# Sliding-window scores of two heads per matmul: 64x64 tiles, queries spread block-diagonally, and one buffer of exponentials

## The chip, the cores and the metric

The kernel runs on one core of one Trainium2 chip. A core has a matrix engine (TensorE, "PE" in the profile, with its weight loads "PEld"), VectorE ("DVE"), ScalarE ("ACT"), GpSimd ("POOL") and SyncE ("SP", which issues most DMAs). Each engine runs its own list of instructions in order and waits on semaphores for the others. Matrix products land in PSUM, eight banks of 512 float32 columns on 128 partitions; all else lives in SBUF. The metric is the time of one execution in microseconds on the device; the time before is the median of three runs.

## The reference

Two attention blocks read the same input `x` (2048 positions, 1024 features, 32 heads of 32) and are mixed by a gate per position:

```python
g = sigmoid((x * gate_w).sum(-1, keepdims=True))
# block A: linear attention; phi(t) = where(t > 0, t + 1, exp(t)) + 1e-6
kv = einsum("bhsd,bhse->bhde", phi(k), v);  z = phi(k) summed over positions
a  = (phi(q) @ kv) / (phi(q) . z + 1e-6)            # then @ A_wo
# block B: each position looks at W = 8 positions, 2 apart, back from itself
logits = q . k[pos - 2*w] * 32**-0.5                # -1e9 where pos - 2*w < 0
b  = softmax(logits) @ v[pos - 2*w]                 # then @ B_wo
out = g * a + (1 - g) * b
```

The change lies in block B, in the product of queries and keys ahead of the softmax.

## The kernel before

The kernel builds a list of operations (`P.op`: engine, function, modelled cost, tiles read and written) and a planner orders it. The planner (`schedule`) runs through modelled time: on each engine it takes, among the operations that are ready, the one with the lowest priority number, which mostly is the order of the program's text. A read-out of PSUM marked "any" (`move`) goes to whichever of ScalarE and VectorE would finish it first by the model. The whole plan is made six times, each with PSUM banks chosen by the plan before, and the one with the shortest modelled span is kept. The order on each engine is then fixed; semaphores follow from the tiles that operations share.

Positions are stored so that even and odd ones form two halves of 1024 (`HS`), so that the window of every second position becomes a window of eight neighbours. The stages, in order of TensorE: values of block B for all positions, written to HBM (`vB_hbm`); queries and keys of block B (`qT`, `kT`, features on partitions, four heads of 32 on the 128 partitions of each of eight chunks), first for one half of the positions, then for the other; key features of block A (`pkS`, `phi`); the products of key features with `x` (line 1628, into `mT`) and from them the state of block A (`state`, line 1607); query features, the fold of the state into the output weights (`fold`, line 1655); and last the output products (line 1700), one tile of 128 positions after another.

The sliding window is worked off beside these stages, in 18 fills (nine of each half of the positions). A fill covers 114 queries (112 in the last of a half) as two sets of `nq` = 57 or 56; each set has its own 64 keys, on partitions 0 to 63 and 64 to 127 of the result. `slot` is called after each main group of eight full matmuls and starts a fill each fifth time (`FILL` = 0.2); the fill's values follow at least three slots later (`PVLAG`). A fill is this:

- two DMAs bring the values of its keys into `vt`;
- `s_fn`, the scores: for each of eight chunks, two sets and four heads one matmul of 32 rows (the head's features), 64 columns (keys) and 57 moving columns (queries), 64 in all, head `j` of a chunk into bank `SO[j]`, that is PSUM banks 4 to 7;
- ScalarE takes the exponential of all four banks into `E` (one of two buffers, `Er`), VectorE multiplies `E` by a mask that keeps the eight keys of each query;
- `values`: 64 matmuls of 64 rows, 32 columns, 57 moving columns from `E` into banks 4 and 5, and after the third chunk eight matmuls with a matrix of ones, 456 moving columns each, for the sums of the softmax, into banks 6 and 7;
- the sums' reciprocal by ScalarE (logarithm, then exponential), and VectorE's product, which overwrites the fill's own queries in `qT`.

Since scores, values and sums all use banks 4 to 7, a fill's scores wait until VectorE has read the result of the fill before. The main groups have banks 0 to 3 (0 to 2 from line 1596 on). [...]

Of the kernel before, what the change touches and what calls it, by code (L numbers as in the profile page):

```python
# [6 lines left out]
ACT = mybir.ActivationFunctionType  # L7
ALU = mybir.AluOpType
AX = mybir.AxisListType
BF16 = mybir.dt.bfloat16  # L10
F32 = mybir.dt.float32
# [1108 lines left out]
def build_kernel(nc, A_x, A_wqkv, A_wo, B_x, B_wqkv, B_wo, gate_w, out):  # L1120
    del B_x
    S = A_x.shape[1]
    NT = S // 128
    HS = S // 2
# [6 lines left out]
    def SB(shape, dtype, name, at=None):  # L1131
        n = SZ[dtype]
        for d in shape[1:]:
            n *= d
        if at is None:
            at = base[0]
            base[0] += (n + 31) // 32 * 32
        uid[0] += 1
        h = nc.alloc_sbuf_tensor_at("%s_%d" % (name, uid[0]), list(shape), dtype, offset=at)
        return Tile("S", h, at, list(shape), dtype)  # L1140
# [48 lines left out]
    def hb(p0, p1, half):  # L1189
        return [("H%d" % half, p0, p1, None)]  # L1190

    xT = SB([128, 8, S], BF16, "xT")
    qT = SB([128, 8, S], BF16, "qT")
    kT = SB([128, 8, S], BF16, "kT")
# [16 lines left out]
    zb = SB([128, 1024], BF16, "zb")  # L1211
    denr = Ring([SB([128, H], F32, "den%d" % i) for i in range(2)])
    mx4 = SB([128, 3], F32, "mx4")
    mx1 = SB([1, 3], F32, "mx1")
    flag = SB([1, 1], I32, "flag")
    zs = SB([128, 16], F32, "zs")
# [4 lines left out]
    vst = Ring([SB([128, 512], BF16, "vst%d" % i) for i in range(8)])  # L1221
    top_ = base[0]
    base[0] = ph
    Er = Ring([SB([128, 32 * 57], BF16, "E%d" % i) for i in range(2)])
    Lr = Ring([SB([128, 2, 4 * 57], F32, "L%d" % i) for i in range(2)])
    vr = Ring([SB([128, 1024], BF16, "v%d" % i) for i in range(3)])
    mtmp = [SB([128, 2, 57], BF16, "mt%d" % i, at=vr.t[2].lo + 256 * i) for i in range(2)]
# [27 lines left out]
    act = lambda n: 0.19 + n / 1200.0  # L1255
    dps = lambda n: 0.14 + n / 960.0

    def plan(seen):

        P = Prog(nc, nc.alloc_semaphore)  # L1260
# [23 lines left out]
        def C(eng, fn, cost, writes, reads=()):  # L1284
            return P.op(eng, fn, cost, reads=reads, writes=writes, prio=-1)

        C("pool", lambda e: e.memset(ones[:], 1.0), 0.1, [ones.all()])
        for i, (n, offs) in enumerate(KINDS):
            for h, o in enumerate(offs):
                m = mtmp[h]  # L1290
                b0 = o + 64 * h
                C("pool", lambda e, m=m: e.memset(m[:], 1.0), 0.1, [m.all()])

                C("pool", lambda e, m=m, n=n, b0=b0: e.affine_select(out=m[:, :, 0:n], in_=m[:, :, 0:n], compare_op=ALU.is_ge, fill=0.0, base=b0,
                                                                     pattern=[[0, 2], [1, n]], channel_multiplier=-1), 0.3, [m.all()], [m.all()])
                C("pool", lambda e, m=m, n=n, b0=b0: e.affine_select(out=m[:, :, 0:n], in_=m[:, :, 0:n], compare_op=ALU.is_ge, fill=0.0, base=7 - b0,
                                                                     pattern=[[0, 2], [-1, n]], channel_multiplier=1), 0.3, [m.all()], [m.all()])
                C("dve", lambda e, m=m, n=n, h=h, i=i: e.tensor_copy(msk[i][64 * h:64 * h + 64, :, :], m[64 * h:64 * h + 64, :, 0:n]), 0.2, [msk[i].all()], [m.all()])
                P.ops[-1].prio = 1100
# [100 lines left out]
        for t, half, lo, hi in [p for q in steps for p in q]:  # L1400
# [6 lines left out]
            if hi < 8:  # L1407
# [4 lines left out]
                 writes=[hb(t * 128, (t + 1) * 128, half)], chan="vst%d" % vs, lat=0.5, prio=5)  # L1412
# [15 lines left out]
        SO = banks[4:8]  # L1428
        main = Pool(banks[0:4])
        todo = []  # L1430
        later = []
        masks = []
        slot_n = [0]

        def fill(e_, qs, nq, offs):
            t0 = e_ * HS
            k0 = [qs + nq * h - offs[h] for h in range(2)]
            m = msk[KINDS.index((nq, offs))]
            vt, vslot = vr.next()
            for h in range(2):  # L1440
                P.op("sp", lambda e, h=h: e.dma_start(vt[64 * h:64 * h + 64, :], vB_hbm[t0 + k0[h]:t0 + k0[h] + 64, :]), 0.4,
                     reads=[hb(t0 + k0[h], t0 + k0[h] + 64, i) for i in range(2)], writes=[vt.all()], chan="v%d_%d" % (vslot, h), lat=0.5)

            def s_fn(e):
                for c in range(8):
                    for h in range(2):
                        for j in range(4):
                            last = e.matmul(SO[j].ap(c * nq, (c + 1) * nq)[64 * h:64 * h + 64, :], kT[32 * j:32 * j + 32, c, t0 + k0[h]:t0 + k0[h] + 64],  # L1448
                                            qT[32 * j:32 * j + 32, c, t0 + qs + h * nq:t0 + qs + (h + 1) * nq], start=True, stop=True, tile_position=(32 * j, 64 * h))
                return last  # L1450
            P.op("pe", s_fn, 0.65, mode="r", reads=[kT.part((0, 8), (t0 + k0[0], t0 + k0[1] + 64)), qT.part((0, 8), (t0 + qs, t0 + qs + 2 * nq))],
                 writes=[s.iv for s in SO], name="S")
            E, _ = Er.next()
            P.op("act", lambda e: e.activation(E[:, 0:32 * nq].rearrange("p (j q) -> p j q", j=4), ps[:, 4:8, 0:8 * nq], ACT.Exp), act(32 * nq),  # L1454
                 reads=[s.iv for s in SO], writes=[E.all()])
            ev = lambda: E[:, 0:32 * nq].rearrange("p (g q) -> p g q", g=16)
            mk = P.op("dve", lambda e: e.tensor_tensor(ev(), ev(), m[:, :, :].rearrange("p r q -> p (r q)")[:, None, :].to_broadcast([128, 16, 2 * nq]), ALU.mult),  # L1457
                 0.15 + 32 * nq / 1920.0, reads=[E.all(), m.all()], writes=[E.all()])
            masks.append(mk)

            def values():

                def each(e):
                    for c in range(8):
                        for j in range(4):
                            for h in range(2):
                                hd = 4 * c + j
                                last = e.matmul(SO[h].ap(c * nq, (c + 1) * nq)[32 * j:32 * j + 32, :], vt[64 * h:64 * h + 64, hd * 32:hd * 32 + 32],  # L1468
                                         E[64 * h:64 * h + 64, (8 * j + c) * nq:(8 * j + c + 1) * nq],
                                         start=True, stop=True, tile_position=(64 * h, 32 * j))  # L1470
                        if c == SUMS_AT:
                            for j in range(4):
                                for h in range(2):
                                    e.matmul(SO[2 + h].ap(0, 8 * nq)[32 * j:32 * j + 32, :], ones[64 * h:64 * h + 64, 0:32],  # L1474
                                             E[64 * h:64 * h + 64, 8 * j * nq:8 * (j + 1) * nq],
                                             start=True, stop=True, tile_position=(64 * h, 32 * j))
                    return last
                bi = [s.iv for s in SO]
                P.op("pe", each, 0.66, mode="c", reads=[vt.all(), ones.all(), E.all()], writes=bi, name="PV")
                for g in range(2):  # L1480
                    L, _ = Lr.next()
                    pb = lambda o, g=g: ps[:, 4 + 2 * o:6 + 2 * o, 4 * g * nq:4 * (g + 1) * nq]
                    P.op("act", lambda e, L=L, pb=pb: e.activation(L[:, :, 0:4 * nq], pb(1), ACT.Ln), act(8 * nq), reads=[SO[2].iv, SO[3].iv], writes=[L.all()])
                    P.op("act", lambda e, L=L: e.activation(L[:, :, 0:4 * nq], L[:, :, 0:4 * nq], ACT.Exp, scale=-1.0), act(8 * nq), reads=[L.all()], writes=[L.all()])  # L1484
                    P.op("dve", lambda e, L=L, pb=pb, g=g: e.tensor_tensor(  # L1485
                        qT[:, 4 * g:4 * g + 4, t0 + qs:t0 + qs + 2 * nq].rearrange("p c (h q) -> p h c q", h=2),
                        pb(0).rearrange("p h (c q) -> p h c q", c=4), L[:, :, 0:4 * nq].rearrange("p h (c q) -> p h c q", c=4), ALU.mult), dps(8 * nq),
                        reads=[SO[0].iv, SO[1].iv, L.all()], writes=[qT.part((4 * g, 4 * g + 4), (t0 + qs, t0 + qs + 2 * nq))])
            after(PVLAG, values)
# [12 lines left out]
        def after(n, f, cols=False):  # L1502
            later.append((slot_n[0] + n, f, cols))
            later.sort(key=lambda x: x[0])
# [245 lines left out]
    for _ in range(PASSES):  # L1750
        got = plan(seen)
        seen = got[2]
        if best is None or got[0].span < best[0].span:
            best = got
    P, flag_op = best[:2]
# [40 lines left out]
def bass_gated_mix__linear_attn_block__sliding_local_dilated__prompt_kernel(nc, A_x, A_wqkv, A_wo, B_x, B_wqkv, B_wo, gate_w, out):  # L1796
    return build_kernel(nc, A_x, A_wqkv, A_wo, B_x, B_wqkv, B_wo, gate_w, out)
# [28 lines left out]
```

## Time and profile before

| | |
|---|---|
| median of three runs | 486.28 us (486.14 to 486.35) |
| profiled execution | 485.35 us, of which the span is 483.5 us |
| granted TensorE clock | 1.0 |
| TensorE busy | 480.0 us, 99% of the span |
| VectorE, ScalarE, GpSimd busy | 294.9, 146.9, 39.4 us |
| score groups | 18, between 125.2 and 306.2 us |

A row of the time line gives start, length, engine, line of the kernel, operation, output and inputs, shape and count; a row of a group gives busy time, mean duration in ns, and the idle time before it with what ended it. Shapes of matmuls read rows*columns of the array, then partitions x moving columns. A matmul's end is modelled, so a chain of TensorE pieces is best priced from start to start. Neighbouring instructions of a line are merged in one row.

### The profile page before, as it was taken

To read this page: it belongs to the slowest core of one execution; us is meant where nothing else is said; L and a number is where in the kernel's file an instruction comes from. 1 tells how busy PE (TensorE), PEld (TensorE's weight loads), DVE (VectorE), ACT (ScalarE), POOL (GpSimd) and SP (SyncE) were. 2 spreads that over 40 slices of the span, in tenths; PEclk is the share of its full clock that TensorE was granted. 3 is DMA by queue.
4 is the path that set the end of the run, shared out by engine and by line. 5 is a ranking of instruction groups with operands and counts; after the bars stand their busy time and mean duration, and the time that the engine had idled before them with its cause. 6 is when DMAs were issued, how large, how long until landed. Compare 5 with 4: busy or idle time off the path is not lost.

```text
span 483.5 us, 10963 instructions
## 1 busy us (share of the span) xinstructions
PE 480.0 (99%) x4882; PEld 229.0 (47%) x4882; DVE 294.9 (61%) x490; ACT 146.9 (30%) x229; POOL 39.4 (8%) x40
## 2 busy tenths in 40 slices
PE   9999999999999999999999999999999999999997
PEld 6444444444444444444455555444444444444444
DVE  2212186799777778766733222489987777767522
ACT  2111111112344446666654356264222000011000
POOL 3000000000000000000015757010000000000000
DMA  8999996223100032013004340571234111122111
GB/s 243 203 190 322 340 342 188 81 94 107 26 23 26 25 110 73 27 34 111 24 25 122 129 104 4 132 197 24 65 89 87 45 43 45 44 66 66 45 45 48
DMA packets 73977, 48.51 MB, mean 100 GB/s; under 512 B 38337, under 2 KB 67394, under 8 KB 73922
## 3 DMA queue, kind: packets, MB, share of 16 engines
q1 hardware_dynamic: 73090, 46.94, 35.5%
q10 hardware_dynamic: 832, 0.79, 0.8%
q8 instruction: 40, 0.66, 0.6%
q14 instruction: 15, 0.12, 0.1%
HBM read 30.41 MB, written 8.39 MB: 80 GB/s over the span
## 4 chain that ended last, share of the span: by engine, by line
PE 99%; DVE 0%; issue 0%
PE ps_all L1349 58%; PE ps_all L1700 23%; PE ps_all L1628 12%; PE ps_all L1448 2%; PE ps_all L1468 2%; PE ps_all L1385 1%; PE ps_all L1474 1%; PE ps_all L1607 1%; PE ps_all L1655 0%; DVE o L1379 0%
## 5 line engine op out<-in xcount | busy, mean ns | idle before, releaser
L1349 PE MATMUL ps_all<-w,xT 128*128 128x512 bf16 x512 | 112.9, 379 | 0.0
L1349 PE MATMUL ps_all<-xT,w 128*128 128x512 bf16 x512 | 112.2, 379 | 0.0
L1349 PEld LDWEIGHTS ps_all<-xT,w 128*128 128x128 bf16 x512 | 49.3, 98 | 58.7
L1349 PEld LDWEIGHTS ps_all<-w,xT 128*128 128x128 bf16 x512 | 49.0, 98 | 57.6
L1355 ACT ACTIVATE e<-ps_all 128x512 bf16<-128x512 f32 x64 | 38.2, 597 | 109.5 <-PE ps_all L1349 108.7
L1700 PE MATMUL ps_all<-w,qT 128*128 128x512 bf16 (+1 forms) x264 | 60.7, 373 | 0.0
L1700 PE MATMUL ps_all<-kT,aT 128*128 128x512 bf16 (+1 forms) x264 | 60.7, 373 | 0.0
L1349 PE MATMUL ps_all<-kT,xT 128*128 128x512 bf16 x256 | 57.9, 379 | 0.0
L1628 PE MATMUL ps_all<-pk,xn 128*128 128x512 bf16 x256 | 57.8, 380 | 0.0
L1700 PEld LDWEIGHTS ps_all<-w,qT 128*128 128x128 bf16 x264 | 25.8, 98 | 29.6 <-issue 0.2
L1700 PEld LDWEIGHTS ps_all<-kT,aT 128*128 128x128 bf16 x264 | 25.8, 98 | 29.4
L1349 PEld LDWEIGHTS ps_all<-kT,xT 128*128 128x128 bf16 x256 | 24.7, 98 | 30.0 <-issue 0.7
L1376 DVE CAST vst<-ps_all 128x512 bf16<-128x512 f32 x16 | 11.1, 692 | 45.4 <-PE ps_all L1349 45.4
L1628 PEld LDWEIGHTS ps_all<-pk,xn 128*128 128x128 bf16 x256 | 23.9, 98 | 27.4
L1379 DVE TENSOR_SCALAR o<-ps_all,gm 128x512 bf16<-128x512 f32 (+1 forms) x27 | 19.7, 731 | 28.0 <-PE ps_all L1700 28.0
L1356 DVE TENSOR_SCALAR e<-e 128x512 bf16<-128x512 bf16 x64 | 18.8, 296 | 27.5 <-ACT e L1355 27.2
L1454 ACT ACTIVATE E<-ps_all 128x1824 bf16<-128x1824 f32 (+1 forms) x18 | 30.4, 1688 | 15.8 <-PE ps_all L1448 15.1
L1457 DVE TENSOR_TENSOR E<-E,msk 128x1824 bf16<-128x1824 bf16 (+1 forms) x18 | 19.8, 1103 | 23.3 <-ACT E L1454 23.3
L1590 POOL TENSOR_TENSOR zacc<-zacc,pk 128x1024 f32<-128x1024 f32 x15 | 32.0, 2130 | 16.5 <-DVE E L1457 15.7
L1485 DVE TENSOR_TENSOR qT<-ps_all,L 128x456 bf16<-128x456 f32 (+1 forms) x36 | 21.2, 625 | 19.4 <-ACT L L1484 19.2
L1377 ACT ACTIVATE kT<-ps_all 128x512 bf16<-128x512 f32 x25 | 14.2, 599 | 33.6 <-PE ps_all L1349 33.6
L1377 ACT ACTIVATE vst<-ps_all 128x512 bf16<-128x512 f32 x16 | 9.6, 597 | 48.7 <-PE ps_all L1349 48.7
(63 smaller groups left out, 361.0 us busy)
## 6 DMA issues: line engine op xcount, KB each, us to landing
v<-vB_hbm SPq DMA_DIRECT2D x36, 128.0 KB, 2.6
vB_hbm<-vst SPq DMA_DIRECT2D x32, 128.0 KB, 4.9
w<-in_B_wqkv_dram SPq DMA_DIRECT2D x4, 1024.0 KB, 8.4
xt<-in_A_x_dram SPq DMA_DIRECT2D x16, 256.0 KB, 5.3
w<-in_A_wqkv_dram SPq DMA_DIRECT2D x4, 1024.0 KB, 9.7
xn<-in_A_x_dram SPq DMA_DIRECT2D x8, 512.0 KB, 3.7
out_dram<-o SPq DMA_DIRECT2D x15, 256.0 KB, 2.1
kT<-in_A_wqkv_dram SPq DMA_DIRECT2D x2, 1024.0 KB, 5.6
```

The costliest lines, as they stand in the source:

```text
L1349: last = e.matmul(bank.ap(), lhs(dc), rhs(dc), start=(dc == 0), stop=(dc == 7))
L1355: P.op("act", lambda e: e.activation(e_[:, :], bank.ap(), ACT.Exp), act(512), reads=[bank.iv], writes=[e_.all()])
L1356: P.op("dve", lambda e: e.tensor_scalar(e_[:, :], e_[:, :], 1.0, 1e-6, op0=ALU.min, op1=ALU.add), 0.25, reads=[e_.all()], writes=[e_.all()])
L1376: fd = lambda e: e.tensor_copy(dst, src())
L1377: fa = lambda e: e.activation(dst, src(), ACT.Copy)
L1379: fd = lambda e: e.tensor_scalar(dst, src(), scale, None, op0=ALU.mult)
L1454: P.op("act", lambda e: e.activation(E[:, 0:32 * nq].rearrange("p (j q) -> p j q", j=4), ps[:, 4:8, 0:8 * nq], ACT.Exp), act(32 * nq), rea ...
L1457: mk = P.op("dve", lambda e: e.tensor_tensor(ev(), ev(), m[:, :, :].rearrange("p r q -> p (r q)")[:, None, :].to_broadcast([128, 16, 2 * n ...
L1485: P.op("dve", lambda e, L=L, pb=pb, g=g: e.tensor_tensor(qT[:, 4 * g:4 * g + 4, t0 + qs:t0 + qs + 2 * nq].rearrange("p c (h q) -> p h c q" ...
L1590: P.op("pool", lambda e, t=t: e.tensor_tensor(zacc[:, :], zacc[:, :], pkS[:, t, :], ALU.add), 2.2, reads=[src, zacc.all()], writes=[zacc.a ...
L1628: last = e.matmul(bank.ap(), tl[:, t, cs:cs + 128], pkS[:, t, r * 512:(r + 1) * 512], start=(t == 0), stop=(t == NT - 1))
L1700: last = e.matmul(bank.ap(0, f1 - f0), lh[:, k, t * 128:(t + 1) * 128], w[:, k, f0:f1], start=(first and k == 0), stop=(not first and k == 7))
```

## The change

A matmul now takes two heads at once: 64 rows (the features of two neighbouring heads), 64 columns (keys), 114 moving columns. So that the two heads are not added up, the queries are first spread into a buffer `qx` of two layers: layer 0 holds the queries with the odd heads of each pair set to zero, layer 1 with the even heads set to zero. The moving operand is the 57 queries of a set from layer 0 and then the same 57 from layer 1, two runs, so one matmul gives the scores of both heads, side by side. There are 32 such matmuls a fill, on four tiles of 64x64.

The spreading (`spread`) is a copy by ScalarE with a scale per partition (column 0 of `pick`, ones and zeros) and a multiplication by VectorE (column 1 of `pick`), each of 8 x 114 columns on 128 partitions. It is put into the list right after the mask of the fill before, and for a fill that has none before it, ahead of its own scores. `qx` is one buffer. Its size is that of one `E`, and `Er` has one buffer instead of two. The heads lie in another order in `E` and in the score banks (pair of heads, chunk, head of the pair): the values' matmuls read other addresses, and the sums' moving operand is eight runs of 57 columns instead of one of 456. The modelled cost of a score group goes from 0.65 to 0.6 us. `pick` is made once, by five memsets on VectorE.

```diff
-    Er = Ring([SB([128, 32 * 57], BF16, "E%d" % i) for i in range(2)])
+    Er = Ring([SB([128, 32 * 57], BF16, "E")])
+    qx = SB([128, 2, 8, 2 * 57], BF16, "qx")
...
+        C("dve", lambda e: e.memset(pick[:, :], 0.0), 0.1, [pick.all()])
+        P.ops[-1].prio = 1100
+        for i in range(4):
+            C("dve", lambda e, i=i: e.memset(pick[32 * i:32 * i + 32, i % 2:i % 2 + 1], 1.0), 0.1, [pick.all()], [pick.all()])
+            P.ops[-1].prio = 1100
...
+        ready = []
+
+        def spread(e_, qs, nq, offs):
+            ready.append((e_, qs))
+            rd = [pick.all(), qT.part((0, 8), (e_ * HS + qs, e_ * HS + qs + 2 * nq))]
+            to = lambda i: qx[:, i, :, 0:2 * nq]
+            of = lambda: qT[:, :, e_ * HS + qs:e_ * HS + qs + 2 * nq]
+            P.op("act", lambda e: e.activation(to(0), of(), ACT.Copy, scale=pick[:, 0:1]), act(16 * nq), reads=rd, writes=[qx.part((0, 1), (0, 8), (0, 114))])
+            P.op("dve", lambda e: e.tensor_scalar(to(1), of(), pick[:, 1:2], None, op0=ALU.mult), 0.1 + 16 * nq / 1920.0, reads=rd, writes=[qx.part((1, 2), (0, 8), (0, 114))])
...
+            if (e_, qs) not in ready:
+                spread(e_, qs, nq, offs)
...
-                        for j in range(4):
-                            last = e.matmul(SO[j].ap(c * nq, (c + 1) * nq)[64 * h:64 * h + 64, :], kT[32 * j:32 * j + 32, c, t0 + k0[h]:t0 + k0[h] + 64],
-                                            qT[32 * j:32 * j + 32, c, t0 + qs + h * nq:t0 + qs + (h + 1) * nq], start=True, stop=True, tile_position=(32 * j, 64 * h))
+                        for g in range(2):
+                            last = e.matmul(SO[2 * g + c // 4].ap(c % 4 * 2 * nq, (c % 4 + 1) * 2 * nq)[64 * h:64 * h + 64, :], kT[64 * g:64 * g + 64, c, t0 + k0[h]:t0 + k0[h] + 64],
+                                            qx[64 * g:64 * g + 64, :, c, h * nq:(h + 1) * nq], start=True, stop=True, tile_position=(64 * g, 64 * h))
...
+            if todo:
+                spread(*todo[0])
...
-                                         E[64 * h:64 * h + 64, (8 * j + c) * nq:(8 * j + c + 1) * nq],
+                                         E[64 * h:64 * h + 64, (j // 2 * 16 + 2 * c + j % 2) * nq:(j // 2 * 16 + 2 * c + j % 2 + 1) * nq],
...
-                                             E[64 * h:64 * h + 64, 8 * j * nq:8 * (j + 1) * nq],
+                                             E[64 * h:64 * h + 64, j // 2 * 16 * nq:(j // 2 + 1) * 16 * nq].rearrange("p (c s q) -> p c s q", c=8, s=2)[:, :, j % 2, :],
```

More of the change, by code (lines that the diff above doesn't have):

```diff
@@ L1213, in build_kernel @@
     mx4 = SB([128, 3], F32, "mx4")
+    pick = SB([128, 2], F32, "pick")
     mx1 = SB([1, 3], F32, "mx1")
@@ L1446, in s_fn @@
                     for h in range(2):
-                        for j in range(4):
-                            last = e.matmul(SO[j].ap(c * nq, (c + 1) * nq)[64 * h:64 * h + 64, :], kT[32 * j:32 * j + 32, c, t0 + k0[h]:t0 + k0[h] + 64],
-                                            qT[32 * j:32 * j + 32, c, t0 + qs + h * nq:t0 + qs + (h + 1) * nq], start=True, stop=True, tile_position=(32 * j, 64 * h))
-                return last
-            P.op("pe", s_fn, 0.65, mode="r", reads=[kT.part((0, 8), (t0 + k0[0], t0 + k0[1] + 64)), qT.part((0, 8), (t0 + qs, t0 + qs + 2 * nq))],
-                 writes=[s.iv for s in SO], name="S")
+                        for g in range(2):
+                            last = e.matmul(SO[2 * g + c // 4].ap(c % 4 * 2 * nq, (c % 4 + 1) * 2 * nq)[64 * h:64 * h + 64, :], kT[64 * g:64 * g + 64, c, t0 + k0[h]:t0 + k0[h] + 64],
+                                            qx[64 * g:64 * g + 64, :, c, h * nq:(h + 1) * nq], start=True, stop=True, tile_position=(64 * g, 64 * h))
+                return last
+            P.op("pe", s_fn, 0.6, mode="r", reads=[kT.part((0, 8), (t0 + k0[0], t0 + k0[1] + 64)), qx.all()], writes=[s.iv for s in SO], name="S")
             E, _ = Er.next()
```

## The prediction

> **What bounds the kernel now.** I read the page's head and section 1 first, then the chain that ended last, then the time line of TensorE around one score group. In order, from the page (busy time by engine, the chain's shares) and from the chain in order of time (start, length, what; the rows of the first two score groups, of one sums group, and of the last score group):
>
> ```profile
> span 483.5 us, 10963 instructions
> PE 480.0 (99%) x4882; PEld 229.0 (47%) x4882; DVE 294.9 (61%) x490; ACT 146.9 (30%) x229; POOL 39.4 (8%) x40
> ...
> PE 99%; DVE 0%; issue 0%
> PE ps_all L1349 58%; PE ps_all L1700 23%; PE ps_all L1628 12%; PE ps_all L1448 2%; PE ps_all L1468 2%; PE ps_all L1385 1%; PE ps_all L1474 1%; PE ps_all L1607 1%; PE ps_all L1655 0%; DVE o L1379 0%
> ```
>
> ```profile
> 6.18 119.14 PE ps_all L1349 x552
> 125.32 0.63 PE ps_all L1448 x64
> ...
> 131.44 0.19 PE ps_all L1474 x8
> ...
> 137.25 0.63 PE ps_all L1448 x63
> ...
> 305.75 0.63 PE ps_all L1448 x63
> ```
>
> TensorE never waits for another engine: the chain is 99% PE, and VectorE (61%) and ScalarE (30%) only matter when they make it wait. So the change is worth what it takes from, or adds to, the TensorE stream, plus any stall it creates. The first row of the chain also prices a full matmul with 512 columns: 119.14 / 552 = 0.216 us.
>
> The score group (line 1448) occurs 18 times. The chain's 0.63 us rests on modelled ends, so I price it by starts. TensorE's time line around the first group, then two narrower windows of it, one for the matmuls that start early and one for those that start late (start, length, what, count):
>
> ```profile
> 124.94 0.38 PE L1349 MATMUL ps_all<-xT,w 128*128 128x512 bf16 x1
> 125.25 0.70 PE L1448 MATMUL ps_all<-qT,kT 32*64 32x57 bf16 x64
> 125.88 0.39 PE L1349 MATMUL ps_all<-xT,w 128*128 128x512 bf16 x1
> ```
>
> ```profile
> 125.25 0.33 PE L1448 MATMUL ps_all<-qT,kT 32*64 32x57 bf16 x32
> ```
>
> ```profile
> 125.48 0.47 PE L1448 MATMUL ps_all<-qT,kT 32*64 32x57 bf16 x32
> ```
>
> ```profile
> L1448 PE MATMUL ps_all<-qT,kT x1152: 181/207/211, 125.2 to 306.2; 32*64 32x57 bf16 x172, 32*64 32x56 bf16 x20
> ```
>
> From the last full matmul to the next is 125.88 - 124.94 = 0.94 us; less that matmul's own 0.216 us, a group costs 0.724 us. It splits into 0.094 us before its first matmul (125.25 - 124.94 - 0.216); 0.49 us from first to last start (125.25 + 0.70 - 0.21); and 0.14 us from the last start to the next full matmul. The narrow windows show why the middle is long: the first 32 matmuls have all started by 125.25 + 0.33 - 0.19 = 125.39, in 0.14 us; then nothing starts until 125.48; the other 32 then start over 0.26 us, about 8 ns apart. (1152 / 64 = 18 groups; the last column of the row gives the times of the first and the last.)
>
> **The change part by part.**
>
> *Half the matmuls, twice the columns.* A group becomes 32 matmuls of 114 columns, on four tiles of 64x64 instead of eight of 32x64. Two groups in the trace say what 32 pairs of weight load and matmul cost, and what a long stream on such tiles costs: the key-value state (32 pairs, four tiles) and the fold (16 tiles, 512 columns).
>
> ```profile
> 258.65 0.38 PE L1607 MATMUL ps_all<-mT,w 128*32 128x32 bf16 x32
> 258.96 0.39 PE L1628 MATMUL ps_all<-pk,xn 128*128 128x512 bf16 x1
> ```
>
> ```profile
> 320.05 0.43 PE L1655 MATMUL ps_all<-kT,kvT 32*32 32x512 bf16 x16
> 320.41 0.39 PE L1349 MATMUL ps_all<-kT,xT 128*128 128x512 bf16 x1
> ```
>
> ```profile
> L1607 PE MATMUL ps_all<-mT,w x256: 176/176/190, 258.7 to 314.7; 128*32 128x32 bf16 x128
> ```
>
> Thirty-two pairs show no second, slow half: the state's last start is at 258.65 + 0.38 - 0.18 = 258.85, 0.20 us after its first. So I expect the 0.09 us hole and the 8 ns pace to go, and the tiles' streaming to set the time. The sums (line 1474 above) stream 456 columns on eight tiles at once in 0.19 us, so 114 columns hold a tile for a quarter, 0.0475 us. Each tile gets eight matmuls, eight rounds. What a round costs beyond its streaming is not shown for this shape. Low end: nothing, as for the sums. High end: the first half of the present group, four rounds of 57 columns (0.024 us) in 0.14 us, has three steps of 0.14 - 0.02 = 0.12 us between first starts, 0.040 us a step, so 0.015 us beyond streaming; the state, with 0.20 / 8 = 0.025 us a round for 32 columns (0.013 us), lies inside that. I take 0.002 us, nearest to the sums since the new stream is long enough to lie over the next weight load, and 0.005 us once for the first round.
>
> - Start: 0.094 us, as now. The 32 starts: 7 x 0.0495 + 0.005, and 0.012 us for the three further starts of the last round (0.14 / 32 = 4 ns each): 0.36 us.
> - Last stream 0.0475 us, then the way out. Now that is 0.14 - 0.024 = 0.116 us, in the state 258.96 - 258.85 - 0.013 = 0.097 us; I take 0.11 us.
> - Sum: 0.094 + 0.36 + 0.0475 + 0.11 = 0.61 us against 0.724 us: 0.114 us less a group, 18 x 0.114 = **2.1 us less**. With no cost per round and the short way out it is 0.58 us a group (2.6 us less); with 0.015 us per round, 0.70 us (0.5 us less).
>
> [...]
>
> *Reading order in the sums and values.* The sums' moving operand becomes eight runs of 57 columns instead of one run of 456; the scores' becomes two runs. No row shows a TensorE operand in runs. Between nothing and a doubled stream I take nothing, since the nearest row, the sums at 0.19 us, reads the very same elements, only in another order; the doubling is a rival. The values (line 1468) change only in addresses: nothing.
>
> *Spreading the queries.* New for each fill: one ScalarE copy and one VectorE multiplication, 8 x 114 = 912 elements each, both off TensorE. Rows (line, engine, operation, count, busy us, mean ns):
>
> ```profile
> L1454 ACT ACTIVATE E<-ps_all 128x1824 bf16<-128x1824 f32 x16 | 27.1, 1691 | 13.9 <-PE ps_all L1448 13.3
> L1380 ACT ACTIVATE qT<-ps_all 128x512 bf16<-128x512 f32 x14 | 8.4, 597 | 34.4 <-PE ps_all L1349 34.4
> L1380 ACT ACTIVATE o<-ps_all,gm 128x512 bf16<-128x512 f32 x6 | 4.1, 688 | 16.0 <-PE ps_all L1700 16.0
> L1356 DVE TENSOR_SCALAR e<-e 128x512 bf16<-128x512 bf16 x64 | 18.8, 296 | 27.5 <-ACT e L1355 27.2
> L1680 DVE TENSOR_TENSOR pn<-p,den 128x512 bf16<-128x512 bf16 x32 | 21.5, 684 | 0.3
> ```
>
> ScalarE: (1691 - 597) / (1824 - 512) = 0.83 ns an element, so 597 + 400 x 0.83 + 91 (a scale by column: 688 - 597) = 1.02 us. VectorE: between 0.30 us (line 1356, no more than 512 elements) and 1.22 us (line 1680's rate); I take 0.5 us. That is 18.4 and 9 us on engines that are 30% and 61% busy. Nothing on the path, as long as two covers hold:
>
> ```profile
> 207.65 3.63 PE L1349 MATMUL ps_all<-w,xT 128*128 128x512 bf16 x16
> ...
> 207.79 1.69 ACT L1454 ACTIVATE E<-ps_all 128x1824 bf16<-128x1824 f32 x1
> ...
> 209.59 0.60 ACT L1355 ACTIVATE e<-ps_all 128x512 bf16<-128x512 f32 x1
> ...
> 210.86 0.69 DVE L1358 SCALAR_TENSOR_TENSOR pk<-ps_all,e 128x512 bf16<-128x512 f32 x1
> ```
>
> ```profile
> 333.71 0.53 PEld L1700 LDWEIGHTS ps_all<-kT,aT 128*128 128x128 bf16 x3
> ```
>
> ```profile
> aT<-pn SPq DMA_TRANSPOSE x16, 3.1
> ```
>
> ```profile
> 328.52 1.23 SPq L1685 DMA_TRANSPOSE aT<-pn  x1
> ```
>
> First, the PSUM banks. The key features' exponential at 209.59 follows a score exponential that held ScalarE from 207.79 for 1.69 us; its bank, filled by the group begun at 207.65, is read out by 210.86 + 0.69 = 211.55. With four banks it is written again four groups of 8 x 0.216 = 1.73 us later, at 214.6 or after, 3 us to spare. A copy of 1.02 us put ahead of it uses a third of that. If that cover were gone, each fill would cost up to 1.02 us. Second, the long chain from the last mask through the sums of key features (GpSimd, three DMAs) to the first transposed numerator: it lands at 328.52 + 3.1 = 331.6 and is wanted at 333.71, 2.1 us to spare, and a VectorE instruction of at most 1.22 us ahead of that mask fits.
>
> *The new wait.* A score group now waits for the spread queries, and all of TensorE is queued behind it. The spread of the next fill can begin when the present score group has ended (one buffer), that is at 125.88; ScalarE first does its 1.69 us exponential, then the copy: ready by about 128.8, and the next score group starts at 137.25. VectorE is ready earlier. Cost nothing.
>
> *One buffer of exponentials; the picking columns.* Scores, values and their read-out share four PSUM banks, so a second score group already can't start before the values that read the first exponentials (137.25 lies after the sums at 131.44): nothing. Five small memsets on VectorE before any value group: nothing.
>
> The sum: -2.1 us. The profiled execution took 485.35 us (its span of 483.5 us and 1.85 us around it), 0.93 us below the median of 486.28 us: 483.2 us for such a profile, **484.2 us** for the median.
>
> **The rivals.**
> 1. *Runs stream slower* (the other side). If TensorE reads a moving operand in short runs at a fraction of its speed, scores and sums both pay: 8 x 0.0475 + 0.19 = 0.57 us of streaming a fill, 10.3 us in 18. The gain is lost when streaming is 20% slower; at half speed it is 10.3 - 2.1 = 8.2 us slower, 494.5 us. For it: no row shows such an operand. Against: each run is 57 neighbouring elements.
> 2. *Columns count, pairs don't.* If the present middle of 0.49 us stayed and 0.19 us of streaming came on top, a group would cost 0.91 us: 18 x 0.19 = 3.4 us slower, 489.7 us. Against: 32 pairs in the state group start in 0.20 us. [...]
> 3. *The gain is eaten by waits.* The planner places 36 more instructions and may move read-outs between ScalarE and VectorE; one late bank or a late numerator costs TensorE 1 to 2 us: 485.3 to 486.3 us, no change to speak of. For it: key features keep ScalarE busy 30.68 of 47 us (row below), and the numerator has 2.1 us to spare. Against: not one wait of TensorE now.
> 4. *More than forecast.* No cost per round, and a score group placed beside a state group, as at 258.65, saving one change of tiling (0.1 us) or two: 483.4 us.
>
> ```profile
> 197.00:244.00 47.00, 47.00 (x863) 23.26 (x842) 32.04 (x59) 30.68 (x47) 0.00 (x0) 1.00 0.15 48
> ```
>
> **How the numbers follow.** A measurement tells 0.2%, about 1 us, from no change. Forecast, with gains of 1.0 to 2.6 us: 0.72; rival 4: 0.08; rival 3, with rounds near the high end: 0.10; rival 1: 0.06; rival 2: 0.04. Faster 0.80, same 0.10, slower 0.10. The range runs from 483.4 us (rival 4) to 485.7 us (rounds at the high end, 0.5 us gained), leaving out the slower rivals and the worst of rival 3.
>
> **What would show it.** Right: score groups of 32 matmuls, 64*64 with 114 columns, about 0.83 us from the last full matmul to the next (now 0.94), with no hole in the middle; the sums still 0.19 us; no wait of TensorE for the spread queries; ScalarE's copy near 1.0 us, VectorE's between 0.3 and 1.2. Wrong: a score group over 0.94 us, sums over 0.19 us, full matmuls more than 0.216 us apart behind a ScalarE or VectorE release, above all between 180 and 250 us or at the first output group.

## The result, and the profile after

The changed kernel takes 484.53 us (median of nine runs), the kernel before 486.14 us beside it: a ratio of 0.9971, with a 95% interval of 0.9961 to 0.9981, that is 0.9 to 1.9 us less. The forecast was 484.2 us, 2.1 us less, in a range of 483.4 to 485.7 us.

From the page of the changed kernel (head, busy time by engine, the chain's shares), and from its groups the two spreadings and the loads and matmuls of the scores (line, engine, operation, count, busy us, mean ns, idle before):

```profile
span 483.1 us, 9788 instructions
PE 472.1 (98%) x4241; PEld 227.2 (47%) x4306; DVE 304.8 (63%) x514; ACT 162.1 (34%) x246; POOL 39.4 (8%) x40
...
PE 98%; issue 1%; DVE 0%
```

```profile
L1449 ACT ACTIVATE qx<-qT,pick 128x912 bf16<-128x912 bf16 x16 | 16.7, 1047 | 1.9 <-DVE qT L1386 1.9
L1467 PE MATMUL ps_all<-qx,kT 64*64 64x114 bf16 x512 | 9.6, 212 | 0.0
L1450 DVE TENSOR_SCALAR qx<-qT,pick 128x912 bf16<-128x912 bf16 x16 | 8.1, 506 | 10.4 <-PE ps_all L1467 10.4
L1467 PEld LDWEIGHTS ps_all<-qx,kT 64*64 64x64 bf16 x576 | 8.1, 105 | 7.6 <-issue 4.7 <-DVE mx L1315 2.1 <-DVE e L1363 0.4
```

TensorE is still the chain. Its "issue" share of 1% is not a wait: there are 4306 weight loads and 4241 matmul records, and each gap is one full matmul long with its weight load present, so 65 records are missing from the trace. Where that matters below I read the loads.

The span shrank by 0.4 us only, and by this one profile the change would seem to have done little. The two ends of the chain in order of time tell why (start, length, what); before, then after:

```profile
0.84 5.33 PE ps_all L1385 x50
...
480.93 0.48 DVE o L1379
```

```profile
0.85 6.00 PE ps_all L1392 x50
...
479.81 0.48 DVE o L1386
```

The 50 warm-up matmuls took 6.00 us in this execution and 5.33 us in that one. The change touches nothing in them; in the profiles of the experiments they took 4.9 to 6.2 us. The other end differs as well: from the start of the last read-out to the end of the span it is 483.5 - 480.93 = 2.6 us before and 483.1 - 479.81 = 3.3 us after (2.6 to 3.0 us in the experiments), when only the last results' way out is left. So I compare executions from their first score group to VectorE's last read-out. Before that is 480.93 - 125.25 = 355.68 us. After, the time line around the first score group reads:

```profile
125.60 0.38 PE L1356 MATMUL ps_all<-xT,w 128*128 128x512 bf16 x1
125.91 0.60 PE L1467 MATMUL ps_all<-qx,kT 64*64 64x114 bf16 x32
126.45 0.39 PE L1356 MATMUL ps_all<-xT,w 128*128 128x512 bf16 x1
```

and the stretch is 479.81 - 125.91 = 353.90 us: **1.78 us less**. A score group now costs 126.45 - 125.60 - 0.216 = 0.63 us instead of 0.724 us; by the starts in nanoseconds it is 0.627 against 0.728 us in both traces' undisturbed groups, and 18 x 0.101 = 1.8 us. That is all of it: value groups, state groups and folds stand as before, within some 0.005 us each (value loads run from 143.09 to 143.82 before and from 143.56 to 144.29 after, 0.73 us in both).

### The profile page after: what moved, and what is told of

It is laid out like the page before. It is cut to its first block, busy times and chain, and to the rows that moved or that the text cites. A ratio compares the mean times of both kernels' runs of the same rounds, so it can differ in the third digit from the quotient of the medians.

```text
span 483.1 us, 9788 instructions
## 1 busy us (share of the span) xinstructions
PE 472.1 (98%) x4241; PEld 227.2 (47%) x4306; DVE 304.8 (63%) x514; ACT 162.1 (34%) x246; POOL 39.4 (8%) x40
## 4 chain that ended last, share of the span: by engine, by line
PE 98%; issue 1%; DVE 0%
PE ps_all L1356 57%; PE ps_all L1720 23%; PE ps_all L1648 11%; PE ps_all L1467 2%; PE ps_all L1488 2%; PE ps_all L1392 1%; PE ps_all L1494 1%; PE ps_all L1627 1%; PE ps_all L1675 0%; DVE o L1386 0%
## 5 line engine op out<-in xcount | busy, mean ns | idle before, releaser
L1356 PE MATMUL ps_all<-w,xT 128*128 128x512 bf16 x493 | 109.5, 379 | 2.4 <-issue 2.1
L1356 PE MATMUL ps_all<-xT,w 128*128 128x512 bf16 x497 | 110.1, 379 | 1.6 <-issue 1.3
L1648 PE MATMUL ps_all<-pk,xn 128*128 128x512 bf16 x242 | 55.5, 379 | 1.7 <-issue 1.4
```

What stands on the lines that cost most here:

```text
L1356: last = e.matmul(bank.ap(), lhs(dc), rhs(dc), start=(dc == 0), stop=(dc == 7))
L1648: last = e.matmul(bank.ap(), tl[:, t, cs:cs + 128], pkS[:, t, r * 512:(r + 1) * 512], start=(t == 0), stop=(t == NT - 1))
```

## The experiments

My theory, A: a tiled group is fed quickly for its first 32 pairs of weight load and matmul, and slowly after that (in the score group of the kernel before, 0.14 us for the first 32, then a hole of 0.1 us and 8.3 ns a pair); the change gains because a score group now has no more than 32 pairs, and the rest of the change costs nothing as long as two covers hold. The rivals: part of the gain comes from the plan or is lost in it; or columns and tiles, not pairs, set the time. Times of the stretch are from each run's first score group to its last read-out, as above.

### All but the matmuls

The spreading, its wait and the one buffer are put into the kernel before; the scores stay 64 matmuls of 57 columns.

```diff
-            P.op("pe", s_fn, ..., reads=[kT..., qT...], ...)        # before
+            P.op("pe", s_fn, ..., reads=[kT..., qT..., qx.all()], ...)   # and spread(), pick, qx, one E
```

> The kernel before with everything of the change but its matmuls: the queries are spread (ScalarE and VectorE), the scores wait for them, the exponentials have one buffer; the scores still go as 64 matmuls of 57 columns on 32x64 tiles, from the unspread queries. Theory A (the whole gain lies in the score group): 0.73 us a group as before, time within 0.2% of before (486.1 us). Rival B (part of the gain, or a hidden loss, lies in the plan, the new wait or the buffer): 0.5 to 1.5 us off, one way or the other, with full matmuls more than 0.216 us apart where it is lost.

486.23 us, ratio to before 1.0004 (0.9996 to 1.0013). The stretch is 481.84 - 126.15 = 355.69 us, before 355.68 us, and the score groups cost 0.728 us each. So 19 us of ScalarE's and some 9 us of VectorE's work, the new wait and the single buffer cost nothing, and none of the gain is theirs. This is what theory A said.

### 64 pairs again, on the new tiles

```diff
-                        for g in range(2):
-                            last = e.matmul(... 2 * nq columns ..., qx[64 * g:64 * g + 64, :, c, h * nq:(h + 1) * nq], ...)
+                        for s in range(2):
+                            for g in range(2):
+                                last = e.matmul(... nq columns ..., qx[64 * g:64 * g + 64, s, c, h * nq:(h + 1) * nq], ...)
```

> The changed kernel with each score matmul split in two, one head (57 columns) each: the same tiles, weights, columns and bytes, but 64 pairs of weight load and matmul instead of 32. Theory A (a group is fed slowly from its 33rd pair on: 0.23 us after the first start, then 8.3 ns a pair): 0.49 us from first to last start, 0.09 + 0.49 + 0.02 + 0.1 = 0.71 us a group against 0.63 us, so 1.4 us of the gain of 1.6 us goes: 486.0 us. Rival B (columns on four tiles set the time): 16 rounds of 0.024 to 0.026 us, 0.39 to 0.41 us from first to last start, time as the changed kernel, 484.5 us.

486.55 us, ratio 1.0016 (1.0007 to 1.0025). Its first group on TensorE's time line:

```profile
125.23 0.38 PE L1356 MATMUL ps_all<-xT,w 128*128 128x512 bf16 x1
125.54 0.74 PE L1468 MATMUL ps_all<-qx,kT 64*64 64x57 bf16 x64
126.21 0.39 PE L1356 MATMUL ps_all<-xT,w 128*128 128x512 bf16 x1
```

0.98 - 0.216 = 0.764 us a group: the gain is gone, and 0.04 us a group more than before is paid. Tiles, weights, columns and zeros are those of the changed kernel; the pairs are twice as many and half as long. The first 38 matmuls have started after 0.31 us; the rest follow at 8.4 ns. Rival B (0.63 us) is out. My 0.71 us was low because the slow part begins later here, after 0.28 us.

This run alone does not single out the slow feed. Ahead of the slow part each of the four tiles already takes 0.032 us for a matmul of 57 columns, as in the 57-column groups further down. Sixteen such rounds would make a group of about 0.73 us (an estimate: 0.093 + 0.51 + 0.123). So of the 0.137 us that a group costs more than in the changed kernel, some 0.10 us come from the shorter matmuls and 0.035 us from the feed. What singles the feed out are groups on eight tiles. In the kernel before, 8.3 ns a pair leave 0.067 us between two matmuls of a tile, twice the 0.032 us that its later rounds take ahead of the hole; and in the next run the same pace holds for all tiles, though half of them get twice as many matmuls as the others.

### 96 pairs on the old tiles

```diff
-                        for j in range(4):
+                        for j in (0, 1, 2, 3, 0, 1):
```

> The kernel before with heads 0 and 1 of each chunk computed twice into the same place: 96 pairs a score group, on the same eight tiles. Theory A (fed slowly from the 33rd pair): 0.23 + 63 x 0.0083 = 0.755 us from first to last start, 0.99 us a group, 18 x 0.26 = 4.7 us slower than before (1.0%). Rival B (rounds on a tile set the time): the busiest tiles have 16 matmuls at 0.031 us, 0.50 us from first to last start, as before: no change.

490.65 us, ratio 1.0108 (1.0093 to 1.0123). The loads of its first group:

```profile
125.24 0.86 PEld L1448 LDWEIGHTS ps_all<-qT,kT 32*64 32x64 bf16 x96 [0.42 <-issue]
126.14 0.11 PEld L1349 LDWEIGHTS ps_all<-xT,w 128*128 128x128 bf16 x2
```

The last load starts 0.86 - 0.10 = 0.76 us after the first, as 0.23 + 63 x 0.0083 says, and the run is 4.8 us slower, forecast 4.7. From the 34th pair to the 96th the loads follow one another at 8.3 ns without a gap. What feeds them at that pace the trace doesn't show, and no run separates the loads from the matmuls of the pairs. Why it is the first 32 pairs that start fast, why the pace is 8.3 ns behind them, and where the hole of about 0.1 us between comes from, stays open.

### One run of 114 columns

```diff
-    qx = SB([128, 2, 8, 2 * 57], BF16, "qx")
+    qx = SB([128, 8, 2, 2 * 57], BF16, "qx")
...
-                                            qx[64 * g:64 * g + 64, :, c, h * nq:(h + 1) * nq], ...
+                                            qx[64 * g:64 * g + 64, c, h, 0:2 * nq], ...
```

> The changed kernel with the spread queries laid out so that the moving operand of a score matmul is one run of 114 columns instead of two of 57. If the two runs cost the extra 1.3 ns a round (0.0508 us against 0.0495 us), the starts span 0.382 us instead of 0.391 us and 18 groups save 0.16 us, too little for the time to show: 484.4 us. If runs cost nothing: 0.391 us. ScalarE's and VectorE's spreading may take longer with shorter runs (1.05 and 0.51 us in the changed kernel), off the path either way.

483.85 us, ratio 0.9968 (0.9956 to 0.9981): the same as the changed kernel. The stretch is 479.10 - 125.25 = 353.85 us, 0.05 us less than there; the starts span 0.387 us instead of 0.391 us. Two runs cost about half a nanosecond a round, less than I allowed. The sums of the changed kernel, in eight runs, leave a value group within some 0.005 us of the 0.82 us before. So rival 1 of the prediction is out.

### 57 columns, and a loss of 5 us

Layer 0 alone, and a memset of VectorE for the places left out.

```diff
-                            ... (c % 4 + 1) * 2 * nq ... qx[64 * g:64 * g + 64, :, c, h * nq:(h + 1) * nq], ...
+                            ... (c % 4 * 2 + 1) * nq ... qx[64 * g:64 * g + 64, 0, c, h * nq:(h + 1) * nq], ...
...
+            P.op("dve", lambda e: e.memset(... odd heads of E ..., 1.0), 0.6, writes=[E.all()])
```

> The changed kernel with layer 0 of the spread queries alone: 32 pairs on 64x64 tiles with 57 columns; the scores of the odd heads are left out (their exponentials are set to one by a memset of VectorE), so half of the scores are missing. Theory A (a round lasts as long as its columns, but not less than the load of the next 64 weight columns, 0.027 us, and the first round has its own load in front): starts span 0.027 + 0.024 + 6 x 0.029 + 0.012 = 0.24 us, the group 0.093 + 0.24 + 0.024 + 0.095 = 0.45 us, 18 x 0.175 = 3.1 us less than the changed kernel: 481.3 us. Rival B (32 pairs cost what 32 pairs cost, whatever they stream): 0.63 us a group, 484.5 us.

491.16 us, ratio 1.0111 (1.0093 to 1.013): slower, where both theories had it no slower. The score groups did what A said: full matmuls at 125.69 and 126.37 around the first, 0.47 us a group against 0.45 forecast. (A's 0.027 us for a load is an estimate, 64 columns at 0.216 / 512 us; in the trace of the changed kernel the loads of a group's first two rounds start 0.028 us apart.) The loss lies elsewhere. TensorE's time line, two rows from the stretch in which it is lost, then that stretch's busy times and granted clock:

```profile
315.37 0.44 PE L1676 MATMUL ps_all<-kT,kvT 32*32 32x512 bf16 x16 [2.13 <-DVE p L1365]
316.57 3.46 PE L1356 MATMUL ps_all<-kT,xT 128*128 128x512 bf16 x8 [0.76 <-ACT kT L1384]
```

```profile
316.00:319.60 3.60, 3.03 (x8) 1.03 (x8) 3.33 (x5) 1.00 (x2) 0.00 (x0) 0.60 1.18 315
```

TensorE waits for VectorE's query features (2.13 us) and a read-out of ScalarE (0.76 us), and then runs eight matmuls in 3.46 us instead of 7 x 0.216 + 0.38 = 1.89 us, at a mean granted clock of 0.60. The memset (0.82 us, mean) sits in each fill between the exponential and the mask; with it the planner starts a fill each 11.7 us where it was 10.1 us (key features of block A), the last sum of key features, which waits for a mask, begins at 312.31 instead of 297.84, and the last two fills fall among the query features. So the experiment moved the other path that I had called covered. That the memset is to blame is argued here; the next run takes it out.

### The same without the memset

```diff
-            ... ps[:, 4:8, 0:8 * nq], ACT.Exp)
+            ... ps[:, 4:8, 0:8 * nq], ACT.Exp, scale=0.0)
```

> The changed kernel with layer 0 of the spread queries alone (57 columns, 32 pairs), as in the run before, but with no instruction added to a fill: the exponential reads all places with a scale of zero, so every score counts as zero. Left out: the odd heads' scores and the use of the others. Theory A (the 57-column group costs 0.470 us, as that run's groups did, and its loss of 5 us came from the memset's delay of the fills): 18 x (0.627 - 0.470) = 2.8 us less than the changed kernel, 481.7 us, with the masks at the times of the changed kernel less what the groups save. Rival B (narrow groups themselves upset the plan): again 488 us or more, with the last masks late.

481.29 us, ratio 0.9899 (0.9882 to 0.9915). The stretch is 476.89 - 125.80 = 351.09 us, 2.81 us below the changed kernel's, as forecast. So once pairs are few, columns do cost: the zeros that the spreading adds take 2.8 us, and the change gains 1.8 us in spite of them. The second rival of the prediction had 0.19 us of streaming more a group (8 rounds of 0.0475 us instead of 0.024 us); the 57 columns more cost 0.627 - 0.470 = 0.157 us here.

### The spreading three times over

```diff
+            for _ in range(3):
                 P.op("act", ... qx layer 0 ...)
                 P.op("dve", ... qx layer 1 ...)
```

> The changed kernel with every spreading done three times over into the same buffer: ScalarE 3.1 us and VectorE 1.5 us a fill instead of 1.05 and 0.51. Theory A (three main groups of slack in the PSUM banks cover it): full matmuls stay 0.216 us apart, score groups 0.63 us, time within 0.2% of the changed kernel, 484.5 us. Rival B (the cover is thin): TensorE waits 0.5 to 2 us in the stage of the key features of block A at several fills, 2 to 5 us slower than the changed kernel.

490.75 us, ratio 1.0101 (1.0078 to 1.0124). This goes to rival B, and at 6.2 us above the changed kernel it is more than its 2 to 5 us. The first loss is in the stage that rival B named: TensorE waits 1.08 us for VectorE ahead of a value group at 196.97. The larger one is late. GpSimd's last sum in the changed kernel, then in this run; then TensorE's time line and the stretch's busy times and granted clock in this run:

```profile
297.84 2.13 POOL L1610 TENSOR_TENSOR zacc<-zacc,pk 128x1024 f32<-128x1024 f32 x1 [2.14 <-DVE E L1475]
```

```profile
304.94 2.13 POOL L1611 TENSOR_TENSOR zacc<-zacc,pk 128x1024 f32<-128x1024 f32 x1 [5.01 <-DVE E L1476]
```

```profile
196.97 0.28 PE L1489 MATMUL ps_all<-E,v 64*32 64x57 bf16 x24 [1.08 <-DVE mx L1564]
...
325.67 1.90 PE L1356 MATMUL ps_all<-kT,xT 128*128 128x512 bf16 x8 [0.92 <-ACT kT L1384]
...
332.30 5.31 PE L1356 MATMUL ps_all<-kT,xT 128*128 128x512 bf16 x16 [2.17 <-DVE kT L1383]
```

```profile
333.30:337.00 3.70, 3.70 (x11) 1.30 (x9) 3.67 (x10) 0.00 (x0) 0.00 (x0) 0.54 0.00 0
```

The last sum comes 7.1 us later, the chain to the first numerator with it, and TensorE waits for read-outs that stand on VectorE behind the first product of that chain. Then, at a mean clock of 0.54, the row of 16 full matmuls lasts 5.31 us instead of 15 x 0.216 + 0.38 = 3.62 us: in the stretch of 3.70 us there are nine weight loads, one each 0.41 us, where at 0.216 us a matmul there would be 17. Ahead of that row TensorE had waited for 2.17 us. The wait of 0.92 us by itself had left the eight matmuls behind it at full speed (1.90 us).

### A longer chain, nothing else

```diff
+            for _ in range(3):
                 P.op("pool", lambda e: e.tensor_copy(zb[:, :]..., zr[:, :]...), 1.4, reads=[zr.all()], writes=[zb.all()])
```

> The changed kernel with GpSimd's last copy of the denominator's vector (2.03 us) done three times, 4.06 us more in the chain from the last masks to the first numerator, and nothing else. Theory A (that chain has 1.9 us to spare, and what is over holds TensorE up): 4.06 - 1.9 = 2.2 us slower than the changed kernel or more, as TensorE's clock and the instructions queued behind on VectorE add to it: 486.7 to 490 us, with the wait between 318 and 336 us. Rival B (the chain is not what held up the two slow runs): within 0.2% of 484.5 us.

485.88 us, ratio 0.9999 (0.9989 to 1.0008), and the stretch is 481.24 - 125.45 = 355.79 us, 1.89 us more than the changed kernel's. The copies, and TensorE's time line:

```profile
318.72 6.24 POOL L1601 COPY zb<-zr 128x1024 bf16<-128x1024 bf16 x3 [19.17 <-DMA zr<-z_hbm]
```

```profile
328.20 0.44 PE L1676 MATMUL ps_all<-kT,kvT 32*32 32x512 bf16 x16 [1.77 <-DVE p L1365]
```

6.24 - 2.04 = 4.2 us were added and 1.9 us came out at the end, so some 2.3 us were to spare; one wait of 1.77 us holds nearly all of it, and it is on VectorE's list, not at the numerator: VectorE's first product waits 1.26 us for GpSimd's copy, and the query features that TensorE needs stand behind it. The median is 1.4 us above the changed kernel's, less than the 2.2 us of theory A and more than rival B's 0.2%. That the chain is nearly critical is shown; so is its slack.

### The place of the sums

The sums of a value group behind its first chunk, or behind its fourth, instead of its third; both with the one-run layout.

```diff
-    SUMS_AT = 2
+    SUMS_AT = 0        # and, in the other run, 3
```

> The kernel of the one-run experiment with the eight sums matmuls of a value group put after its first chunk instead of its third. Theory A (the value group's 72 pairs are fed slowly too, so that its end depends on the number of pairs and not on where the long streams lie): 0.82 us a value group, 483.9 us. [...]

> The kernel of the one-run experiment with the sums after the fourth chunk (32 pairs ahead of them, where the first fast stretch ends) instead of the third. Since putting them first cost 0.08 us a value group, the place matters. Theory A (the long streams pay best where the array would otherwise stand waiting for pairs, just behind the first 32): value groups 0.80 us or less, 0.3 us or more gained in all. Rival B (the third chunk is best, as the sums hide the wait that follows): 0.82 to 0.88 us a group, up to 1.1 us lost.

485.74 us and 485.75 us, ratios 0.9995 (0.9985 to 1.0005) and 0.9991 (0.9982 to 1.0001); with the sums behind the third chunk it was 483.85 us. A value group takes 0.90 us in both, against 0.82 us. Both forms of theory A fell: with 72 pairs in each case, the end does depend on where the eight long streams stand, and just behind the first 32 pairs is no better place. In the second run the loss is larger than its rival B allowed (0.88 us a group, 1.1 us in all). With the sums first, TensorE's time line reads

```profile
131.79 0.22 PE L1488 MATMUL ps_all<-E,v 64*32 64x57 bf16 x8
131.83 0.38 PE L1494 MATMUL ps_all<-E,ones 64*32 64x456 bf16 x8
132.03 0.64 PE L1488 MATMUL ps_all<-E,v 64*32 64x57 bf16 x56
132.60 0.39 PE L1356 MATMUL ps_all<-xT,w 128*128 128x512 bf16 x1
```

Behind the sums 24 pairs, eight more than were left of the first 32, start at 3 to 4 ns each, and the slow feed begins after them, 0.43 us from the group's start. So "0.23 us after the first start" holds where the array takes the first 32 pairs at once, and is no rule for groups in which a long stream holds them up. How the feed restarts stays open; neither run tells it.

## Why the prediction was right, and where its sizes were off

- *What bounds the kernel*: right. TensorE's stream is the chain before and after, and the whole difference of 1.78 us lies in 18 score groups.
- *Half the matmuls, twice the columns*: the mechanism was right, and it was the doubtful one: 96 pairs on the old tiles cost what 63 slow pairs cost, and 64 pairs on the new ones lose the gain, though for the larger part by their shorter matmuls. The size was off: 0.627 us a group against 0.61 us forecast and 0.728 us before, a gain of 0.10 us instead of 0.114 us. The term that was mis-sized is the first round. Two narrow windows of TensorE's time line of the changed kernel, the first beginning with the second round, the second with the fourth:

```profile
125.99 0.37 PE L1467 MATMUL ps_all<-qx,kT 64*64 64x114 bf16 x16
```

```profile
126.09 0.41 PE L1467 MATMUL ps_all<-qx,kT 64*64 64x114 bf16 x18
```

  First round 125.99 - 125.91 = 0.08 us, in nanoseconds 77, where I had 0.0545 us; later rounds 0.05 us, as forecast (0.0495, measured 0.0508). The first round is 0.026 us longer than the others. The records of the loads differ there: those of the first round start with its matmuls (125.911 and 125.912 us), those of the second at 125.939 us, 0.050 us ahead of their matmuls; from the third round on a load starts 2 ns behind the matmul before it in the same tile (125.991 and 125.989 us) and lies under it, and a round takes 0.051 us for 0.0475 us of streaming. That the 0.026 us are the first load's, which has no matmul to lie under, is an estimate from these starts; no run shows it by itself. The way out was 0.015 us shorter than I took it, which by luck took back half of what the rounds cost more.

  The kernel before already held the long first round: its first four rounds start at 0, 0.052, 0.084 and 0.115 us. I averaged them to 0.040 us a step; the later ones alone are 0.008 us over their streaming, not 0.015 us. And my sum for the high end was wrong: 0.015 us a round gives 0.706 us a group, 0.3 us gained in all and not 0.5 us.
- *Reading in runs*: right, nothing to speak of (0.05 us in all for the scores; value groups with the sums in runs stay within some 0.005 us each).
- *Spreading*: 1.047 us on ScalarE for 1.02 forecast, 0.506 us on VectorE for 0.5. That it costs nothing is shown by the run with all but the matmuls.
- *The covers*: right for this change, and thinner than "a third of the slack" sounded. Three spreadings instead of one, 2.1 us of ScalarE and 1.0 us of VectorE a fill more, cost 6 us. I had priced the bank's slack at a single fill and put the chain to the first numerator down as 2.1 us to spare; the longer chain measured 2.3 us. That these two agree is chance, since I counted to the numerator's landing and what waited was VectorE's first product, with TensorE behind it. What I had not seen is that longer fills make the planner start them farther apart (in key features mostly 11.8 us instead of 10.1 us with three spreadings), so that the last mask, and the chain behind it, slips by several times what one fill is delayed. Rival 3 did not happen here, but its mechanism is real.
- *The new wait, the single buffer, the memsets*: nothing, as said.
- *Rival 1*: out by the one-run run and the value groups. *Rival 2*: out by the result itself, 0.627 us a group against its 0.91 us. *Rival 4*: no more than the forecast came.

## What to carry to other kernels

Where small matmuls are packed into tiles, count the pairs of weight load and matmul in a group before counting columns: here, where the tiles took the first 32 pairs at once, the 33rd pair and those behind it came at 8.3 ns each after a hole of 0.1 us, and half the array's work on zeros was cheaper than that. Price a group by the starts of the full matmuls around it, not by modelled ends, and look for the second path: work that costs nothing on idle engines may still push the last item of a periodic job, and with it a chain that has only 2 us to spare. To measure such a change in one profile, leave the start and the end of the execution out.

## What the runs showed of the hardware that I had not expected

The same 50 warm-up matmuls took 5.33 us (before), 6.00 us (after), 6.23 us (all but the matmuls) and 5.34 us (one run), up to half of what this change gains; medians of many runs average that out, a single span does not. And after standing still for some microseconds TensorE ran slower in two of the runs. In the 57-column run it waited 2.13 us and, after a fold of 0.44 us, another 0.76 us, and eight full matmuls then took 3.46 us at a mean granted clock of 0.60, against 7 x 0.216 + 0.38 = 1.89 us. With three spreadings a wait of 2.17 us had the same effect (16 full matmuls in 5.31 us, a mean clock of 0.54); in the run with the longer chain a single wait of 1.77 us had none, the clock stayed at 1.00. Where the limit lies no run tells.
